# Second half's normalised tokens turned channel-major on VectorE and through DRAM, where TensorE turned them into PSUM

## The chip, the cores and the metric

The kernel runs on one core of one Trainium2 chip. The metric is device time in microseconds (us) of one execution, taken as the median of several runs; lower is better. In the profile the engines are called PE (TensorE, matrix products; PEld is its weight loading), DVE (VectorE), ACT (ScalarE), POOL (GpSimd) and SP (the sync engine, which here issues all DMAs, in program order). Every engine executes its own instructions strictly in the order in which the program issued them.

## The reference: what is computed

Input: x with 2048 tokens of 576 channels, all in float32. With `xn = layernorm(x)`, the result is

```python
out = x + A(xn, wqkv, wo) + B(xn, w1, b1, w2)
# A: qkv = xn @ wqkv, 32 heads of 18 channels; token s attends to tokens s, s-2, ..., s-14;
#    softmax over these 8 logits; the result @ wo
# B: mish(xn @ w1 + b1) @ w2, hidden width 4608
```

Both branches read the same normalised tokens `xn`. Every product with `xn` as an operand on TensorE needs it channel-major: 128 channels on the partitions, tokens along the free dimension. The input lies in DRAM token-major.

## The kernel before, in words

**Precision.** TensorE multiplies a reduced float format (fp32r in the profile). Each float32 operand is split into a high part (a cast by ACT) and a low part (the operand minus its high part, by DVE or POOL), and products are made as high·high + high·low + low·high. So for `xn` there are two channel-major copies, high and low, in one tile `XTs[hf, b]`.

**Tiling.** The tokens are taken in two halves (`hf` 0 and 1) of 1024; a half has two blocks (`b` 0 and 1) of 512 tokens, a block has four tiles (`jj`) of 128 tokens. Tile n = 4b + jj. The 576 channels are four groups of 128 (`KT` = 4) and a rest of 64. The rest is put twice into a 128-row group, so that its high part and its low part can share one operand; block 1 also needs the difference `rem` between the rests of block 0 and block 1, since some of the products are made by a seven-product scheme that works on sums and differences of blocks (`s_step`, `s_high` and `s_low` make these sums, tiles `S0` to `S2`; the sums run on POOL).

**The order of work.** TensorE's work is written out by hand as a list of slots, `plan`. A slot is one item for TensorE:

- `m`: a part of the up-projection of one pair of hidden groups q (0 to 17);
- `p`: a chunk of the down-projection, 24 products (L767), whose four results DVE adds to an accumulator (L771);
- `q`: 14 products that give one token tile's q, k and v for a group of heads (L348);
- `z`: the same for two groups of heads at once, by the seven-product scheme (L446);
- `t`: the turn of one tile of the second half (`ln_transpose(1, b, jj)`);
- `o`: the output projection.

Everything else is hung in front of a slot with `before(slot, function)`. In a slot the hung functions are issued first, in the order in which the program registered them, then mish of the part before, then TensorE's item. So a slot fixes the place of an instruction in its engine's queue, not its time. Attention runs on POOL (products L533 and L571) and DVE (sums L538 and L577), in steps hung in front of slots too.

**The turn of the second half, before.** Its tiles are loaded (`x_load`, L105) while the first half's last up-projection groups run, normalised by ACT in place (`norm1`, L139), and the rest of 64 channels is doubled by POOL (L140). In slot `t` TensorE transposes the tile against an identity, four groups of 128 channels into one PSUM bank (L75), the rest into another (L76) and, for block 1, `rem` too (L78). ACT casts from PSUM to the high part (L81, L86), DVE subtracts from PSUM to the low part (L82, L87). Two banks are taken for it: of tag "out" for the first three tiles of block 0 (`pair`), else of tag "h".

**The slots around the change.** E is the slot `t` of tile 3. The first column is the slot, the second TensorE's item, the third when that item began in the profile of before.

| slot | item | us |
|---|---|---|
| E-25 | chunk of q 14 | 471.78 |
| E-23 | first part of q 16 | 476.81 |
| E-21, E-19, E-17, E-15 | chunks of q 15 | 481.34, 485.89, 490.89, 495.89 |
| E-13 | first part of q 17, the last reader of the first half's block 0 | 500.89 |
| E-11, E-9, E-6, E-3 | chunks of q 16 | 505.42, 509.97, 515.54, 521.11 |
| E-8, E-5, E-2, E | `t` of tiles 0 to 3 | 513.15, 518.72, 524.29, 526.69 |
| E+1, E+2 | chunks of q 17 | from 527.15, without a gap |
| E+3, E+5, E+8, E+10 | second half's q items, block 0 | 533.61, 539.55, 546.07, 549.49 |
| E+4, E+6 | chunks of q 17; each chunk of q 17 is followed by two stores of finished accumulators (`y_store`, L1041) | 536.36, 542.31 |
| E+7, E+9, E+11, E+13 | `t` of tiles 4 to 7 | 545.50, 548.92, 552.34, 555.77 |
| E+12, E+14 to E+16 | q items, block 1, tiles 4 to 7 | 552.92, then from 556.35 without a gap |
| E+17 to E+24 | q items of the second group of heads | up to 586.73 |
| E+25 to E+28 | first four z items | 586.73, 589.49, 591.85, 595.29 |

The weights of the z items come by `z_fetch`, hung in front of E+14 to E+25, into buffers that other tiles have left: T2 into the four "raw" buffers, R3 into "r3", B11 and B21 into "acc". The sums `s_step(1, c, k)` are hung in front of E+14 to E+26.

**The way through DRAM that was there.** Attention's output is token-major too and is turned without TensorE: `o_turn` transposes every 32x32 block of a 128x576 tile on DVE (L593), `o_send` stores it by four DMAs in rows of 32 floats, 128 bytes, so that the blocks land in channel-major places (L602), and `o_load` reads it back in rows of 512 bytes (L892).

Of the kernel before, what the change touches and what calls it, by code (L numbers as in the profile page):

```python
# [21 lines left out]
TB = SH // NB  # L22
TJ = SH // P
JB = TJ // NB
KT = D // P
NF = F // P
NP = NF // 2
# [12 lines left out]
def block_kernel(ctx: ExitStack, tc: tile.TileContext, x, wq, wo, w1, b1, w2, mask, out):  # L40
    nc = tc.nc
    tpn = iter(range(1000))

    const = ctx.enter_context(tc.tile_pool(name="const", bufs=1))
    sb = ctx.enter_context(tc.tile_pool(name="sb", bufs=2))
    ps = ctx.enter_context(tc.tile_pool(name="ps", bufs=4, space=bass.MemoryType.PSUM))
    dram = ctx.enter_context(tc.tile_pool(name="dram", bufs=1, space=bass.MemoryType.DRAM))
# [16 lines left out]
    for k in range(30):  # L64
        nc.tensor.transpose(warm[:, (k % 4) * P:(k % 4 + 1) * P], ident, ident)

    def transpose_split(src, dst, col, extra=None, pair=False):
        n = next(tpn)
        if pair:
            ta, tb = (ps.tile([P, 512], F32, tag="out", bufs=4, name=f"tt{k}_{n}") for k in range(2))  # L70
        else:
            ta = ps.tile([P, 512], F32, tag="h", bufs=4, name=f"ta_{n}")
            tb = ps.tile([P, 512], F32, tag="h", bufs=4, name=f"tb_{n}")
        for k in range(KT):
            nc.tensor.transpose(ta[:, k * P:(k + 1) * P], src[:, k * P:(k + 1) * P], ident)  # L75
        nc.tensor.transpose(tb[:, 0:P], src[:, KT * P:(KT + 1) * P], ident)  # L76
        if extra is not None:
            nc.tensor.transpose(tb[:, P:2 * P], extra, ident)  # L78
        tav = ta.rearrange("p (k t) -> p k t", k=KT)
        hi = dst[:, 0:KT, col:col + P]  # L80
        nc.scalar.copy(hi, tav)  # L81
        nc.vector.tensor_sub(dst[:, 5:5 + KT, col:col + P], tav, hi.bitcast(F32))  # L82
        e = 1 if extra is None else 2
        hr = dst[:, KT:KT + 5 * e - 4:5, col:col + P]
        tbv = tb.rearrange("p (k t) -> p k t", k=KT)[:, 0:e]
        nc.scalar.copy(hr, tbv)  # L86
        nc.vector.tensor_sub(hr[64:P], tbv[64:P], hr[64:P].bitcast(F32))  # L87

    XTs = {}
    rems = {}  # L90
    xns = {}
    XNB = 5
# [7 lines left out]
    def x_tile(hf, n):  # L100
        return x[hf * SH:(hf + 1) * SH, :].rearrange("(p j) d -> p j d", j=TJ)[:, n, :]

    def x_load(n):
        xn = sb.tile([P, 5 * P], F32, tag="xn", bufs=XNB, name=f"xn_1_{n}_{next(tpn)}")
        nc.sync.dma_start(xn[:, 0:D], x_tile(1, n))  # L105
        xns[1, n] = xn

# [29 lines left out]
    def norm1(n):  # L137
        xn = xns[1, n]
        nc.scalar.activation(xn[:, 0:D], xn[:, 0:D], AF.Identity, bias=nm1[:, n, :], scale=rs1[:, n, :])  # L139
        nc.gpsimd.tensor_copy(xn[:, D:D + 64], xn[:, KT * P:D])  # L140

    group = {}

    def ln_group(ns):
# [39 lines left out]
    def ln_transpose(hf, b, jj):  # L184
        if jj == 0:
            XTs[hf, b] = sb.tile([P, 9 + b, TB], F32R, tag=f"xt{b}", bufs=1, name=f"xt_{hf}_{b}")
        xn = xns[hf, b * JB + jj]
        if (b, jj) == (0, 0):
            rems[hf] = sb.tile([P, JB, P], F32, tag="tt", bufs=2, name=f"rem_{hf}")
        rem = rems[hf][:, jj, :]  # L190
        if b == 0:
            nc.gpsimd.tensor_copy(rem, xn[:, KT * P:])
        else:
            nc.gpsimd.tensor_tensor(out=rem, in0=rem, in1=xn[:, KT * P:], op=ALU.subtract)
        transpose_split(xn, XTs[hf, b], jj * P, rem if b else None, (hf, b) == (1, 0) and jj < 3)

    def raw_load(src, width, name):
        raw = sb.tile([P, 5 * P], F32, tag="raw", bufs=4, name=f"r{name}")
# [176 lines left out]
    BUFS = {"wb": 3, "wc": 2, "wa0": 1, "a0": 3, "a1": 2, "acc": 9, "raw": 4, "tt": 2, "r3": 1, "mn": 5, "xn": XNB}  # L375
# [767 lines left out]
    at = {}  # L1143
# [3 lines left out]
    def add(tag, *fns, alias=None):  # L1147
        at[tag] = at[alias] = len(plan)
        plan.append((list(fns), [], PART[tag[3]] if tag[0] == "m" else US[tag[0]]))

    def before(i, fn):
        plan[max(i, 0)][1].append(fn)
# [70 lines left out]
            qkv_item(0, 0, 0, n)  # L1223

    def tr(b, jj):
        add(("t", 1, b, jj), lambda: ln_transpose(1, b, jj))

    CHUNKS = ((1, 0), (1, 1), (0, 0), (0, 1))

# [136 lines left out]
    for q in range(1, 2 * OC + 1):  # L1366
        i = spot(0, q, (3,2)[q > 1])
# [5 lines left out]
    i = spot(0, NP - 1, 0)  # L1373
# [5 lines left out]
    i = at["q", 1, 0, 1, 1]  # L1379
# [4 lines left out]
    i = spot(0, 9, 4)  # L1384
    for k in range(2):
        for n, steps in enumerate((
# [42 lines left out]
    i = at["q", 0, 1, 1, 0]  # L1429
# [3 lines left out]
    i = at["q", 0, 3, 1, 0]  # L1433
# [23 lines left out]
        before(i, lambda n=n: x_load(n))  # L1457
        before(i + 5, lambda n=n: stats1(n))
    before(i + 6, var1)
    i = spot(0, NP - 2, 0)  # L1460
    for jj in range(JB):
        before(i + 2 * jj, lambda jj=jj: x_load(jj))
        before(i + 2 * jj + 6, lambda jj=jj: norm1(jj))
        before(at["t", 1, 0, jj] + 2, lambda jj=jj: x_load(JB + jj))
    for jj in range(JB):
        before(at["p", 0, NP - 1, 1, 1] + jj, lambda jj=jj: norm1(JB + jj))

    for n, (name, pr) in enumerate((name, pr) for name in ("P4", "P5", "P2", "P3") for pr in range(2)):
        i = items[dict(P4=0, P5=2, P3=2, P2=3)[name]][2] + pr
# [125 lines left out]
```

## Time and profile before

| | before |
|---|---|
| runs | 1113.94, 1114.05, 1114.44 us, median 1114.05 |
| the profiled execution, whole | 1114.25 us |
| its span, first to last instruction | 1112.5 us |
| granted TensorE clock | 1.0 of full speed |
| share of the span busy: PE, PEld, DVE, ACT, POOL | 99%, 91%, 76%, 45%, 71% |
| DMA: mean rate, share of 16 engines' span | 244 GB/s, 71.6% |

How to read the views that follow: a group of instructions is given as line, engine, operation, output<-input, shape and count, then busy time and mean nanoseconds of one, then idle time of its engine in front of it and who ended it. A timeline row is start, duration, engine, line and a merged run of equal instructions ("x24"), with the wait in front of the run in brackets. TensorE's products are pipelined: the duration of a row reaches past the start of the next one, so what a row costs TensorE is the distance to the next start. Rows of SPq are DMAs being issued. A row of a window lists the length of the stretch, the busy time of each engine in it, the granted clock, the busy share of the DMA engines and what they moved.

### The profile page before, as it was taken

What the parts mean: (1) busy time and instruction counts of PE and PEld (TensorE: products, weight loads), DVE (VectorE), ACT (ScalarE), POOL (GpSimd) and SP (SyncE); (2) the same over time, 40 slices, a digit from 0 to 9 for tenths busy, and PEclk for the clock granted to TensorE, in tenths of its full rate; (3) what the DMA queues carried; (4) which work ended last, traced back from release to release, by engine and by line L of the source; (5) the groups of instructions that cost most, each with busy time, mean ns of one, the idle gap of its engine ahead of it and who ended that gap; (6) DMA issues with size and microseconds to landing.
All of it is one profiled execution on the core that took longest, in us unless ns stands there. A gap on an engine that the chain in (4) does not pass through costs nothing.

```text
span 1112.5 us, 18203 instructions
## 1 busy us (share of the span) xinstructions
PE 1101.6 (99%) x6550; PEld 1015.2 (91%) x6550; DVE 849.5 (76%) x1367; ACT 499.5 (45%) x917; POOL 790.8 (71%) x639
## 2 busy tenths in 40 slices
PE   9999999999999999999999999999999999999998
PEld 8999899999999999999999889989989999999998
DVE  6369788888889888897656577786776677777786
ACT  5544655544454544555333354433433344343353
POOL 2479777766679688785788676666688976867532
PEclk9999999999999999999999999999999999999999
DMA  6899696868777758675597898565664657776574
GB/s 202 283 312 316 225 356 214 285 233 276 258 242 264 268 208 301 249 249 204 190 323 241 245 375 307 211 196 196 220 222 170 209 195 223 244 288 219 171 232 142
DMA packets 178270, 271.60 MB, mean 244 GB/s; under 512 B 53218, under 2 KB 120068, under 8 KB 178180
## 3 DMA queue, kind: packets, MB, share of 16 engines
q1 hardware_dynamic: 178180, 270.44, 71.6%
q8 instruction: 52, 0.85, 0.3%
q14 instruction: 38, 0.31, 0.1%
HBM read 160.39 MB, written 110.00 MB: 243 GB/s over the span
## 4 chain that ended last, share of the span: by engine, by line
PE 87%; POOL 6%; DVE 3%; issue 2%; ACT 1%; DMA 0%; SPq 0%; POOLq 0%; DVEq 0%; ACTq 0%
PE h L669 28%; PE po L767 21%; PE pq L348 9%; PE po L880 9%; PE po L859 6%; PE h L675 5%; PE o L1063 5%; PE z L446 3%; POOL pv L571 2%; POOL accP L868 1%; POOL pr L533 1%; POOL act L721 1%; POOL s L620 1%; DMA acc<-in_x 0%; PE ta L75 0%
## 5 line engine op out<-in xcount | busy, mean ns | idle before, releaser
L767 PEld LDWEIGHTS po<-w,act 128*128 128x128 f32 x1728 | 236.4, 188 | 6.0 <-POOL act L721 0.4
L767 PE MATMUL po<-w,act 128*128 128x288 f32 x1728 | 240.7, 295 | 0.1
L533 POOL TENSOR_TENSOR pr<-q,kv 128x576 f32<-128x576 f32 x128 | 196.9, 1563 | 8.5 <-DMA q<-q_d 5.0
L721 POOL TENSOR_TENSOR act<-c,act 128x512 fp32r<-128x512 f32 x81 | 107.3, 1325 | 128.6 <-ACT act L720 128.6
L571 POOL TENSOR_TENSOR pv<-L,kv 128x576 f32<-128x576 f32 x128 | 177.9, 1484 | 26.1 <-DVE L L564 21.2
L771 DVE TENSOR_TENSOR acc<-po,acc 128x288 f32<-128x288 f32 x288 | 119.4, 448 | 29.9 <-PE po L767 29.0
L348 PE MATMUL pq<-wq,xt 128*128 128x432 f32 x672 | 136.5, 361 | 1.0 <-ACT xt L81 1.0
L880 PEld LDWEIGHTS po<-w,act 128*128 128x128 f32 x960 | 130.9, 188 | 4.6 <-DVE accP L883 1.8
L880 PE MATMUL po<-w,act 128*128 128x288 f32 x960 | 133.5, 295 | 1.0 <-DVE accP L883 1.0
L348 PEld LDWEIGHTS pq<-wq,xt 128*128 128x128 f32 x672 | 125.0, 188 | 8.0 <-ACT xt L81 1.8
L715 ACT ACTIVATE c<-c,b1c 128x512 f32<-128x512 f32 x81 | 58.7, 725 | 140.7 <-DVE c L714 140.4
L669 PE MATMUL h<-xt,t 128*128 128x512 f32 x432 | 110.6, 391 | 0.5 <-DVE rt L714 0.3
L669 PE MATMUL h<-S,t 128*128 128x512 f32 x432 | 110.5, 391 | 0.0
L577 DVE TENSOR_REDUCE og<-pv 128x144 f32<-128x1152 f32 x64 | 86.0, 1345 | 25.7 <-POOL pv L571 25.6
L669 PE MATMUL h<-xt,wa 128*128 128x512 f32 x432 | 104.1, 390 | 0.0
L538 DVE TENSOR_REDUCE L<-pr 128x64 f32<-128x1152 f32 x64 | 85.8, 1341 | 23.8 <-POOL pr L533 23.7
L703 ACT COPY c<-h 128x512 f32<-128x512 f32 x81 | 47.4, 586 | 124.1 <-PE h L675 73.0
L859 PEld LDWEIGHTS po<-pw,u 128*128 128x128 f32 x672 | 92.2, 188 | 5.4 <-DVE u L813 2.1
L859 PE MATMUL po<-pw,u 128*128 128x288 f32 x672 | 94.3, 295 | 2.5 <-DVE u L813 1.6
L669 PEld LDWEIGHTS h<-xt,wa 128*128 128x128 f32 x432 | 80.9, 188 | 17.0
L669 PEld LDWEIGHTS h<-xt,t 128*128 128x128 f32 x432 | 79.0, 188 | 15.7 <-DVE rt L714 0.7
L883 DVE TENSOR_TENSOR accP<-po,accP 128x288 f32<-128x288 f32 x160 | 68.9, 452 | 29.8 <-PE po L880 28.2
(228 smaller groups left out, 1853.8 us busy)
## 6 DMA issues: line engine op xcount, KB each, us to landing
kv<-kv_d SPq DMA_DIRECT2D x64, 396.0 KB, 5.1
kept_t<-t SPq DMA_DIRECT2D x36, 512.0 KB, 4.8
t<-kept_t SPq DMA_DIRECT2D x36, 512.0 KB, 6.7
rw<-in_w SPq DMA_DIRECT2D x36, 320.0 KB, 4.4
kept_wa<-wa SPq DMA_DIRECT2D x18, 640.0 KB, 4.7
kept_w<-w SPq DMA_DIRECT2D x20, 576.0 KB, 4.1
wa<-kept_wa SPq DMA_DIRECT2D x18, 640.0 KB, 5.2
w<-kept_w SPq DMA_DIRECT2D x20, 576.0 KB, 4.1
```

The lines of the kernel that those rows point to most:

```text
L348: nc.tensor.matmul(pq[:, 0:432], XT[:, xi, tok], wt[wi][:, hl, 0:432], start=i == 0, stop=i == len(seq) - 1)
L533: nc.gpsimd.tensor_tensor(out=pr[:, x:x + hh], in0=q[:, j0 + x:j0 + x + hh, None, :].to_broadcast([P, hh, W, CU]), in1=win(kt, 0, CU, j0 + ...
L538: nc.vector.tensor_reduce(L[:, k, j0:j0 + hj].rearrange("p j w h -> p (j w h)"), pr.rearrange("p j w (h d) -> p (j w h) d", h=2), axis=AX, ...
L571: nc.gpsimd.tensor_tensor(out=pr[:, x:x + hj].rearrange("p j d w -> p j w d"), in0=L[:, k, x:x + hj, :, h:h + 1].to_broadcast([P, hj, W, DH]),
L577: nc.vector.tensor_reduce(og[:, c0:c0 + DH, :].rearrange("p d j -> p j d"), pr, axis=AX, op=ALU.add)
L669: nc.tensor.matmul(ph, wt[:, wl, wk * P:(wk + 1) * P], X[:, xs, :], start=first and i == 0, stop=last and i == len(seq) - 1, skip_group_ch ...
L721: nc.gpsimd.tensor_tensor(out=a[:, 1, :], in0=t, in1=a[:, 0, :].bitcast(F32), op=ALU.subtract)
L767: nc.tensor.matmul(po, acts[hf, q, b, j][:, al, tok], done["w2", hf, 2 * q + j][:, wl, c * HC:(c + 1) * HC], start=i == 0, stop=i == 5)
L771: nc.vector.tensor_tensor(out=t, in0=po, in1=t, op=ALU.add)
L859: nc.tensor.matmul(po, units[e, k, qq][:, al, tok], w[:, qq, wl, :], start=i == 0, stop=i == 5)
L880: nc.tensor.matmul(po, acts[hf, q, b, j][:, al, tok], done["w2", hf, 2 * q + j][:, wl, c * HC:(c + 1) * HC], start=i == 0, stop=i == 5)
L883: nc.vector.tensor_tensor(out=t, in0=po, in1=t, op=ALU.add)
```

## The change

The eight `t` slots stay in the list but are empty. A second-half tile n now goes through six steps, each hung in front of a slot of its own:

1. `x_load`: as before, but tiles 4 to 7 go into "raw" buffers.
2. `norm1`: as before, without POOL's copy of the rest.
3. `x_turn`: DVE transposes the 32x32 blocks of the tile (128x576) into one of two buffers, by turns (one in the ninth "acc" buffer, one in "r3").
4. `x_put`: four DMAs store it in rows of 128 bytes in a DRAM tile [576 channels, 128 tokens].
5. `x_back`: one DMA reads the four groups of 128 channels, in rows of 512 bytes, and two more read the rest into both halves of a fifth group; the target is an "xn" buffer.
6. `x_high` and, a slot later, `x_low`: POOL copies the rest (block 0) or subtracts it (block 1) into `rem`; ACT casts from SBUF to the high part; DVE subtracts from SBUF to the low part. For block 1 the group of the rest and `rem` are cast and subtracted one by one.

The slots, relative to E:

| tile | load | norm | turn | put | back | high | low |
|---|---|---|---|---|---|---|---|
| 0 | -25 | -23 | -22 | -20 | -17 | -11 | -10 |
| 1 | -22 | -20 | -19 | -17 | -14 | -9 | -8 |
| 2 | -19 | -17 | -16 | -14 | -11 | -6 | -5 |
| 3 | -16 | -14 | -13 | -11 | -8 | -4 | -3 |
| 4 | -13 | -8 | -7 | -5 | 0 | +4 | +5 |
| 5 | -12 | -5 | -4 | -2 | +2 | +7 | +8 |
| 6 | -10 | -2 | -1 | +1 | +4 | +10 | +11 |
| 7 | -6 | +1 | +2 | +4 | +6 | +12 | +13 |

Before, the loads stood in front of E-23, -21, -19, -17, -6, -3, 0 and +2 and the normalisations in front of E-17, -15, -13, -11 and E+2 to +5. The first half's turns stay on TensorE.

```diff
-    def transpose_split(src, dst, col, extra=None, pair=False):
+    def transpose_split(src, dst, col, extra=None):
...
-        nc.gpsimd.tensor_copy(xn[:, D:D + 64], xn[:, KT * P:D])
+    def x_turn(n):
...
+        t = xTs["ab"[n % 2]]
+        nc.vector.transpose(t, xns[1, n][:, 0:D])
+    def x_put(n):
+        t = xTs[n]
+        d = xT_d[n] = dram.tile([D, P], F32, name=f"xT_d{n}")
+        rows = d.rearrange("(n i) p -> i n p", i=32)
+        for g in range(4):
+            part = slice(g * 32, (g + 1) * 32)
+            nc.sync.dma_start(rows[:, :, part], t[part].rearrange("i (n k) -> i n k", k=32))
+    def x_back(n):
+        xn = xns[1, n] = sb.tile([P, 5 * P], F32, tag="xn", bufs=XNB, name=f"xn_t_{n}")
+        nc.sync.dma_start(xn[:, 0:KT * P].rearrange("p (k t) -> p k t", k=KT),
+                          xT_d[n][0:KT * P].rearrange("(k p) t -> p k t", p=P))
+        for r_ in range(2):
+            nc.sync.dma_start(xn[r_ * 64:(r_ + 1) * 64, KT * P:], xT_d[n][KT * P:D])
+    def x_high(n):
...
+        if b == 0:
+            nc.gpsimd.tensor_copy(rem, xr)
+        else:
+            nc.gpsimd.tensor_tensor(out=rem, in0=rem, in1=xr, op=ALU.subtract)
+        for s_, hi, lo in x_parts(n):
+            nc.scalar.copy(hi, s_)
+    def x_low(n):
+        for k, (s_, hi, lo) in enumerate(x_parts(n)):
+            r_ = slice(64 if k else 0, P)
+            nc.vector.tensor_tensor(out=lo[r_], in0=s_[r_], in1=hi[r_].bitcast(F32), op=ALU.subtract)
...
     def tr(b, jj):
-        add(("t", 1, b, jj), lambda: ln_transpose(1, b, jj))
+        add(("t", 1, b, jj))
...
-    i = spot(0, NP - 2, 0)
-    for jj in range(JB):
-        before(i + 2 * jj, lambda jj=jj: x_load(jj))
-        before(i + 2 * jj + 6, lambda jj=jj: norm1(jj))
-        before(at["t", 1, 0, jj] + 2, lambda jj=jj: x_load(JB + jj))
-    for jj in range(JB):
-        before(at["p", 0, NP - 1, 1, 1] + jj, lambda jj=jj: norm1(JB + jj))
+    i, e = spot(0, NP - 3, 8), at["t", 1, 0, JB - 1]
+    for n in range(TJ):
+        b_, jj = divmod(n, JB)
+        turn = (e - 7, e - 4, e - 1, e + 2)[jj] if b_ else i + 3 * jj + 3
+        load_at = (e - 13, e - 12, e - 10, e - 6)[jj] if b_ else i + 3 * jj
+        split = e + (4, 7, 10, 12)[jj] if b_ else e + (-11, -9, -6, -4)[jj]
+        before(load_at, lambda n=n: x_load(n, "raw" if n >= JB else "xn"))
+        before(turn - 1, lambda n=n: norm1(n))
+        before(turn, lambda n=n: x_turn(n))
+        before(turn + 2, lambda n=n: x_put(n))
+        before(e + (0, 2, 4, 6)[jj] if b_ else turn + 5, lambda n=n: x_back(n))
+        before(split, lambda n=n: x_high(n))
+        before(split + 1, lambda n=n: x_low(n))
```

More of the change, by code (lines that the diff above doesn't have):

```diff
@@ L65, in block_kernel @@
         nc.tensor.transpose(warm[:, (k % 4) * P:(k % 4 + 1) * P], ident, ident)
-    def transpose_split(src, dst, col, extra=None, pair=False):
+    def transpose_split(src, dst, col, extra=None):
         n = next(tpn)
[L69 to L73, printed above, removed]
+        ta = ps.tile([P, 512], F32, tag="h", bufs=4, name=f"ta_{n}")
+        tb = ps.tile([P, 512], F32, tag="h", bufs=4, name=f"tb_{n}")
         for k in range(KT):
@@ L101, in x_tile, with x_load @@
         return x[hf * SH:(hf + 1) * SH, :].rearrange("(p j) d -> p j d", j=TJ)[:, n, :]
-    def x_load(n):
-        xn = sb.tile([P, 5 * P], F32, tag="xn", bufs=XNB, name=f"xn_1_{n}_{next(tpn)}")
+    def x_load(n, tag="xn"):
+        xn = sb.tile([P, 5 * P], F32, tag=tag, bufs=BUFS[tag], name=f"xn_1_{n}_{next(tpn)}")
         nc.sync.dma_start(xn[:, 0:D], x_tile(1, n))
@@ L194, in ln_transpose @@
             nc.gpsimd.tensor_tensor(out=rem, in0=rem, in1=xn[:, KT * P:], op=ALU.subtract)
-        transpose_split(xn, XTs[hf, b], jj * P, rem if b else None, (hf, b) == (1, 0) and jj < 3)
+        transpose_split(xn, XTs[hf, b], jj * P, rem if b else None)
     def raw_load(src, width, name):
```

17 lines of the change are left out of this document (added).

## The prediction

> **What bounds the kernel now.** First the page: the busy shares and the chain of waits.
>
> ```profile
> span 1112.5 us, 18203 instructions
> PE 1101.6 (99%) x6550; PEld 1015.2 (91%) x6550; DVE 849.5 (76%) x1367; ACT 499.5 (45%) x917; POOL 790.8 (71%) x639
> PE 87%; POOL 6%; DVE 3%; issue 2%; ACT 1%; DMA 0%; SPq 0%; POOLq 0%; DVEq 0%; ACTq 0%
> PE po L859 <- DVE u L813: 1.6, 1, 1.6
> ...
> PE h L669 <- DVE c L714: 0.2, 1, 0.2
> ```
>
> TensorE is busy for 99% of the span and is 87% of the chain. The last two lines are the first and the last of the nine rows that list all that TensorE waited for; the longest wait is 1.6 us, none lies at a turn of the second half. So work taken from TensorE shortens the kernel one for one, as long as nothing else comes late.
>
> **What the change removes.** The timeline of TensorE around a turn of block 0 and two of block 1:
>
> ```profile
> 508.60 1.53 PE L669 MATMUL h<-S,t 128*128 128x512 f32 x6
> 509.97 3.34 PE L767 MATMUL po<-w,act 128*128 128x288 f32 x24
> 513.15 0.60 PE L75 MATMUL tt<-ident,xn 128*128 128x128 f32 x4
> 513.58 0.27 PE L76 MATMUL tt<-ident,xn 128*128 128x128 f32 x1
> 513.61 1.63 PE L669 MATMUL h<-S,t 128*128 128x512 f32 x6
> 515.08 0.62 PE L675 MATMUL h<-xt,wc 128*128 128x512 f32 x2
> ...
> 533.61 2.92 PE L348 MATMUL pq<-wq,xt 128*128 128x432 f32 x14
> 536.36 3.35 PE L767 MATMUL po<-w,act 128*128 128x288 f32 x24
> ...
> 539.55 2.92 PE L348 MATMUL pq<-wq,xt 128*128 128x432 f32 x14
> ...
> 546.07 3.01 PE L348 MATMUL pq<-wq,xt 128*128 128x432 f32 x14
> 548.92 0.60 PE L75 MATMUL ta<-ident,xn 128*128 128x128 f32 x4
> ...
> 549.49 3.01 PE L348 MATMUL pq<-wq,xt 128*128 128x432 f32 x14
> ```
>
> Starts are what counts. The five transposes of block 0 hold TensorE from 513.15 to 513.61: 0.46 us. The six products behind them take 515.08 - 513.61 = 1.47, where the same six behind other products took 509.97 - 508.60 = 1.37: 0.10 more. Together 0.56 a tile. In block 1 it is 549.49 - 548.92 = 0.57, and the fourteen products behind a turn take 548.92 - 546.07 = 2.85 against 536.36 - 533.61 = 2.75: 0.67 a tile. Four of each: 4 x 0.56 + 4 x 0.67 = **4.92 us less on TensorE**, 2.24 of them before E+1, 2.68 from E+7 to E+14. No wait of TensorE hangs on them, so nothing further is won.
>
> **What it adds on VectorE.** The groups of the nearest instructions and the busy times by stage:
>
> ```profile
> L255 DVE TENSOR_TENSOR t<-tt,t 128x512 fp32r<-128x512 f32 x36 | 45.1, 1254 | 4.3 <-ACT t L254 4.2
> L593 DVE STREAM_TRANSPOSE oT<-og 128x576 f32<-128x576 f32 x16 | 12.4, 773 | 0.3
> L82 DVE TENSOR_TENSOR xt<-ta,xt 128x512 fp32r<-128x512 f32 x13 | 9.0, 690 | 11.6 <-ACT xt L81 11.5
> L87 DVE TENSOR_TENSOR xt<-tb,xt 64x256 fp32r<-64x256 f32 x8 | 3.4, 428 | 0.2
> L87 DVE TENSOR_TENSOR xt<-tb,xt 64x128 fp32r<-64x128 f32 x5 | 1.5, 294 | 0.2
> ```
> ```profile
> 480.00:500.00 20.00, 20.00 (x130) 18.71 (x129) 19.19 (x29) 8.89 (x15) 17.03 (x15) 1.00 0.82 289
> 500.00:513.00 13.00, 13.00 (x78) 11.82 (x77) 10.67 (x15) 7.88 (x12) 7.64 (x8) 1.00 0.49 182
> 513.00:533.00 20.00, 20.00 (x139) 18.92 (x138) 15.38 (x31) 10.40 (x19) 12.20 (x14) 1.00 0.62 211
> 533.00:556.00 23.00, 23.00 (x145) 22.20 (x144) 13.91 (x22) 6.27 (x17) 16.17 (x17) 1.00 0.60 187
> 556.00:580.00 24.00, 24.00 (x126) 22.95 (x125) 13.29 (x15) 9.68 (x26) 21.11 (x17) 1.00 0.99 328
> 580.00:600.00 20.00, 19.86 (x102) 18.66 (x101) 12.28 (x14) 6.30 (x19) 18.07 (x14) 1.00 1.00 316
> ```
>
> A turn is the same instruction and shape as attention's L593: 0.773 us. The subtraction of four groups moves from PSUM (L82, 0.690) to SBUF. The nearest row from SBUF is L255, 1.254: 0.564 more; the other end is no more at all. The rest costs 2 x 0.294 in block 1 against 0.428.
>
> From 480 to 533, DVE idles 0.81 + 2.33 + 4.62 = 7.76 us; TensorE's 2.24 less shorten that to 5.52. Into it go the turns of tiles 0 to 6, 7 x 0.773 = 5.41, and four subtractions, 0 to 2.26: 5.41 to 7.67 in a room of 5.52. Between -0.1 and 2.15 us do not fit. What is late then is L771, the addition that frees the banks of a down-projection chunk, and TensorE waits for a free bank; the chunks at E+1 and E+2 follow each other without a gap, so it shows there. I take the middle, **+1.0 us**. From 533 on DVE idles 9.09 us, 6.41 after the shortening, and is given 0.77 + 4 x (0.564 + 0.16) = 3.7: nothing. ACT casts what it cast before. A normalisation of block 0 now stands two slots behind its load, where it stood six; a late load stops ACT and the copies behind it that empty the up-projection's banks. ACT idles for 11.1 of the 20 us from 480, which hides that: nothing, and without that cover as much as the load is late.
>
> **What it adds on the DMA queue.** The nearest transfers, attention's store and load of the same shape, a window that held little but one such store, one that held large transfers, and the z stage's last weights:
>
> ```profile
> 482.00:484.75 2.75, 2.75 (x22) 2.71 (x21) 2.75 (x4) 1.54 (x3) 2.75 (x2) 1.00 0.84 117
> 486.00:490.00 4.00, 4.00 (x30) 3.83 (x29) 4.00 (x6) 1.00 (x2) 4.00 (x3) 1.00 1.03 408
> ```
> ```profile
> 481.36 1.98 SPq L602 DMA_DIRECT2D o_d<-oT  x4
> ...
> 584.77 0.90 SPq L421 DMA_DIRECT2D z_T<-kept_T  x2
> ```
> ```profile
> zraw_T<-kept_T SPq DMA_DIRECT2D x4, 216.0 KB, 6.4
> o<-o_d SPq DMA_DIRECT2D x16, 320.0 KB, 5.7
> o_d<-oT SPq DMA_DIRECT2D x64, 72.0 KB, 2.6
> ```
> ```profile
> 593.42 1.34 PE L446 MATMUL z<-z_T,xt 128*128 128x432 f32 x6
> ```
>
> A store of a tile takes SP 1.98 us to issue, lands 2.6 us behind the last issue, and holds the DMA engines for 0.84 x 2.75 = 2.31 us. Reading back moves 320 KB in rows of 512 bytes: 0.8 us at the 408 GB/s of the second window, 2.8 at the 117 of the first. I take 1.0, near the fast end, since these rows are four times as long. Eight tiles: 8 x 3.3 = 26.5 us of DMA time. From 480 to 556 the engines were busy for 16.4 + 6.4 + 12.4 + 13.8 = 49.0 us; with the new work 75.4, in 76 - 4.9 = 71.1 us. Up to 4.3 us spill past E+14, into a stage at a share of 0.99 and 1.00. There the weights T4 are issued at 584.77, land by the 6.4 of their nearest row at 591.2, and TensorE needs them at 593.42: 2.2 us to spare. So TensorE waits there for 0 to 2.1 us.
>
> The same lateness meets a second path: in the chain of waits from 565 to 595 stand POOL's sums L620 for the same z items, which need the tiles of block 1.
>
> ```profile
> 537.97 0.24 POOL L140 COPY xn<-xn 128x64 f32<-128x64 f32 x1 [5.32 <-ACT xn L139]
> ...
> 552.57 1.30 POOL L620 TENSOR_TENSOR s<-xt 128x512 f32<-128x512 f32 x1
> ```
> ```profile
> 569.91 1.36 POOL s L620
> ...
> 595.29 24.82 PE z L446 x125
> ```
>
> POOL loses L140 and its wait of 5.32, so it can be early; but its `rem` of tile 7 now waits for `x_back`. That is issued behind the stores of chunk E+4, which ends at 539.55 - 2.24 = 537.3; an addition later and 2 us of SP make it 540, and 5.7 to land 545.7, with the spill up to 550. The sums began at 552.57 and have to begin 4.9 earlier, at 547.7: 0 to 2.3 us late. Both paths end in the same z items, so they are one term: 0 to 2.3, and I take **+0.6**, since the spill counts every transfer as if none could wait for a gap.
>
> **The sum.** -4.92 + 1.0 + 0.6 = -3.3 us. The profiled execution took 1114.25 us, 0.2 above the median of 1114.05; against the median the forecast is 1110.7. By the lower bounds of both terms 1109.1, by the upper ones 1113.6. About 0.2% (2.2 us) is what this measurement can tell from no change.
>
> [...] TensorE makes a 128x128 block here in about 0.11 us (513.15 to 513.58 for four), DVE only blocks of 32x32 and then a store. [...]
>
> **The rivals.**
>
> *All of the room is found* (chance 0.12): DVE's queue takes the turns in its idle time and the spill finds gaps. For it: from E-13 to E-11 no chunk stands, so lateness there costs nothing. Time: 1109.1.
>
> *Both engines are full* (0.15): subtractions cost 1.254 throughout, as POOL is busy, and the whole spill reaches z. For it: DVE's 19.19 of 20 us at 480. Against: 9 us of its idle time behind 533. Time: 1113.6, within 0.2% of before.
>
> *The round trip holds up SP, slower* (0.22): `x_back` waits in SP's queue until the store in front of it has landed, and everything behind it, y stores, attention's loads and the weights of the q items, waits too. A trip held up by the one before adds 1.98 + 2.6 + about 1.5 = 6.1 us. If that happens once in block 1 on top of the full spill, tile 7 lands at 545.7 + 4.3 + 6.1 = 556.1, 8.4 behind the 547.7 at which POOL's sums must begin, and TensorE waits as long in z: -4.9 + 1.0 + 8.4 = +4.5, 1118.5. It becomes slower than before when tile 7 lands after 552.6. Against: two to five slots lie between each store and its read, so SP seldom meets a store that is still on its way.
>
> *The store breaks into elements* (0.01): one packet of the store takes 2.31 x 16 / 2304 = 16 ns of one DMA engine; at 4 bytes instead of 128 a tile has 32 times as many, 74 us, and the kernel would take over 1600 us. Against: L602 has the same form and its packets are 128 bytes long.
>
> **How the numbers follow.** The forecast keeps 0.50, 1109.1 to 1113.6 with most of it under 1111.8. Faster by over 0.2%: 0.50 + 0.12 = 0.62. Within: 0.15. Slower: 0.22 + 0.01 = 0.23. The range leaves out the upper half of the slow case and the tip of the fast one: 1109.0 to 1117.0.
>
> **What would show it.** Right: no L75 after 500 us; z beginning 3 to 5 us earlier than 586.73; eight DVE transposes at 0.77 us more; waits of L767 at E+1 and E+2 for L771 of about a microsecond; SBUF subtractions between 0.69 and 1.25. Wrong: waits of L348 for the subtraction or the cast, of L446 for POOL, DVE or a DMA above 2.3 us, or a z stage that begins no earlier.

## The result, and the profile after

| | before | after |
|---|---|---|
| median (runs) | 1114.44 us (7: 1113.94 to 1114.96) | 1117.86 us (7: 1116.44 to 1118.22) |
| profiled execution, its span | 1114.25, 1112.5 | 1118.04, 1116.2 |
| TensorE's start into z, and out of it | 586.73, 624.88 | 589.34, 628.24 |

The changed kernel is slower: ratio 1.0029, 95% interval 1.0019 to 1.0039. The forecast was 1110.7 and its range ended at 1117.0. "Out of z" is the start of the first up-projection row behind the z items; it serves below as a cleaner measure than the time, since the stretch behind it holds one more wait, around 820, that varies from run to run; each value is from one profiled execution.

The page of after, and what TensorE waited for between 465 and 640 (total, times, longest). One row is left out, 0.7 us for L749; before has it too, for L703, and nothing else:

```profile
PE 1099.9 (99%) x6506; PEld 1011.8 (91%) x6506; DVE 858.5 (77%) x1379; ACT 499.7 (45%) x921; POOL 790.8 (71%) x631
...
PE po L813 <- DVE acc L817: 2.9, 1, 2.9
PE z L492 <- DVE zqs L505: 0.9, 1, 0.9
PE pq L394 <- DMA wq<-kept_wq: 0.9, 3, 0.4
PE po L813 <- POOL act L767: 0.8, 1, 0.8
```

TensorE's share is still 99%, but 3.8 us of standstill now lie at one place that had none. The timeline of TensorE in before, the last part of the up-projection and the first row behind z:

```profile
526.23 0.62 PE L675 MATMUL h<-xt,wc 128*128 128x512 f32 x2
624.88 2.93 PE L669 MATMUL h<-xt,wa 128*128 128x512 f32 x12
```

And in after, from the last part of the up-projection to the first q item, and at z:

```profile
524.26 0.62 PE L721 MATMUL h<-xt,wc 128*128 128x512 f32 x2
527.83 0.53 PE L813 MATMUL po<-w,act 128*128 128x288 f32 x2 [2.95 <-DVE acc L817]
529.18 7.90 PE L813 MATMUL po<-w,act 128*128 128x288 f32 x46 [0.82 <-POOL act L767]
536.92 3.10 PE L394 MATMUL pq<-wq,xt 128*128 128x432 f32 x14
...
589.34 2.51 PE L492 MATMUL z<-zacc_B,xt 128*128 128x432 f32 x12
598.66 1.43 PE L492 MATMUL z<-z_B,S 128*128 128x432 f32 x6 [0.91 <-DVE zqs L505]
628.24 2.93 PE L715 MATMUL h<-xt,wa 128*128 128x512 f32 x12
```

Before, 7.38 us lay between the last part (526.23) and the first q item (533.61); now 12.66 (524.26 to 536.92). 3.77 of it are the two waits in brackets. A further 1.6 are in the row of 46 products: it took 7.74 us to the next start, where 46 of 48 products take 6.46 x 46/48 = 6.2. The windows show why; the column behind the five engines is the granted clock, 0.88, 0.50 and 0.76:

```profile
528.00:530.00 2.00, 1.18 (x6) 0.94 (x7) 1.77 (x2) 1.97 (x4) 2.00 (x2) 0.88 0.82 246
530.00:532.00 2.00, 2.00 (x10) 2.00 (x10) 0.75 (x2) 0.54 (x1) 2.00 (x3) 0.50 1.06 220
532.00:534.00 2.00, 2.00 (x14) 2.00 (x14) 0.69 (x3) 0.00 (x0) 2.00 (x3) 0.76 0.97 295
```

The whole difference, from starts of TensorE in both timelines: -1.97 us at the last part, +5.28 from there to the first q item, -0.70 over the q items (where the turns of block 1 had stood with 2.68, so some 2.0 were lost again, 0.9 of it in waits for `wq`), +0.75 in z, +0.34 behind it. Together +3.70, as the spans say (1116.2 - 1112.5). So the saving of the turns is there, and more than it is given back at three places.

VectorE, by stage, in the windows whose rows the prediction shows for before:

```profile
533.00:556.00 23.00, 23.00 (x143) 22.17 (x142) 18.23 (x28) 5.77 (x20) 15.01 (x14) 1.00 0.93 261
556.00:580.00 24.00, 23.11 (x115) 20.91 (x114) 19.12 (x18) 8.11 (x23) 21.96 (x17) 1.00 1.06 344
```

From 533 to 556 it was busy for 13.91 us and is now for 18.23, from 556 to 580 for 13.29 and now 19.12. That is 10.1 us more, where the prediction had put 3.7. The subtractions of block 1 make 8.0 of it (12.5 us for its four tiles against 4.5) and a turn 0.8; the rest is other work that came later than before and so fell into these windows. In the timeline of VectorE of before:

```profile
526.12 0.68 DVE L82 TENSOR_TENSOR xt<-tt,xt 128x512 fp32r<-128x512 f32 x1
557.08 0.69 DVE L82 TENSOR_TENSOR xt<-ta,xt 128x512 fp32r<-128x512 f32 x1 [0.90 <-ACT xt L81]
557.80 0.43 DVE L87 TENSOR_TENSOR xt<-tb,xt 64x256 fp32r<-64x256 f32 x1
```

The same in after:

```profile
514.66 1.00 DVE L185 TENSOR_TENSOR xt<-xn_t,xt 128x512 fp32r<-128x512 f32 x2
518.44 2.13 DVE L185 TENSOR_TENSOR xt<-xn_t,xt 128x512 fp32r<-128x512 f32 x2
553.08 3.31 DVE L185 TENSOR_TENSOR xt<-xn_t,xt 128x512 fp32r<-128x512 f32 x2 [0.28 <-ACT xt L180]
556.32 1.38 DVE L185 TENSOR_TENSOR xt<-rem,xt 64x128 fp32r<-64x128 f32 x1
```

Before, the 128x512 subtraction took 0.68 or 0.69 us wherever it stood. Now it and the small one behind it (one row of two, 1.00 at 514.66) take 2.13 at 518.44, and tile 6 takes 3.31 + 1.38, where a tile of block 1 took 0.69 + 0.43. GpSimd's timeline beside the last ones, of before:

```profile
556.44 2.82 POOL L533 TENSOR_TENSOR pr<-q,kv 128x576 f32<-128x576 f32 x2
```

And of after, with the first of its sums for z:

```profile
552.97 3.28 POOL L579 TENSOR_TENSOR pr<-q,kv 128x576 f32<-128x576 f32 x2
556.21 1.34 POOL L666 TENSOR_TENSOR s<-xt 128x512 f32<-128x512 f32 x1
```

GpSimd worked beside the subtraction at 557.08 of before too, and it did not grow. That subtraction read one operand from PSUM; the new ones read both from SBUF. The third thing that is late is a tile; ScalarE's timeline of after, the cast of tile 3:

```profile
523.98 0.82 ACT L180 CAST xt<-xn_t 128x512 fp32r<-128x512 f32 x2 [4.16 <-DMA xn_t<-xT_d]
```

ScalarE and all that is queued on it stood for 4.16 us until the tile had come back from DRAM.

### The profile page after: what moved, and what is told of

Same layout as the page of the kernel before. It is cut to its first block, busy times and chain, and to the rows that moved or that the text cites. A ratio compares the mean times of both kernels' runs of the same rounds, so it can differ in the third digit from the quotient of the medians.

```text
span 1116.2 us, 18218 instructions
## 1 busy us (share of the span) xinstructions
PE 1099.9 (99%) x6506; PEld 1011.8 (91%) x6506; DVE 858.5 (77%) x1379; ACT 499.7 (45%) x921; POOL 790.8 (71%) x631
## 4 chain that ended last, share of the span: by engine, by line
PE 83%; POOL 6%; DVE 6%; issue 3%; ACT 2%; DMA 1%; SPq 0%; DVEq 0%; POOLq 0%; ACTq 0%
PE h L715 27%; PE po L813 20%; PE po L926 9%; PE pq L394 8%; PE po L905 6%; PE h L721 5%; PE o L1109 4%; PE z L492 3%; POOL pv L617 2%; POOL accP L914 1%; DVE xt L185 1%; POOL pr L579 1%; POOL act L767 1%; POOL s L666 1%; DVE L L584 1%
## 5 line engine op out<-in xcount | busy, mean ns | idle before, releaser
L617 POOL TENSOR_TENSOR pv<-L,kv 128x576 f32<-128x576 f32 x128 | 178.1, 1486 | 27.4 <-DVE L L610 22.8
L817 DVE TENSOR_TENSOR acc<-po,acc 128x288 f32<-128x288 f32 x288 | 118.9, 448 | 28.4 <-PE po L813 27.5
L584 DVE TENSOR_REDUCE L<-pr 128x64 f32<-128x1152 f32 x64 | 85.8, 1342 | 25.9 <-POOL pr L579 25.8
L749 ACT COPY c<-h 128x512 f32<-128x512 f32 x81 | 47.4, 585 | 120.2 <-PE h L721 71.2
```

Source lines behind the costliest of these rows:

```text
L584: nc.vector.tensor_reduce(L[:, k, j0:j0 + hj].rearrange("p j w h -> p (j w h)"), pr.rearrange("p j w (h d) -> p (j w h) d", h=2), axis=AX, ...
L617: nc.gpsimd.tensor_tensor(out=pr[:, x:x + hj].rearrange("p j d w -> p j w d"), in0=L[:, k, x:x + hj, :, h:h + 1].to_broadcast([P, hj, W, DH]),
L817: nc.vector.tensor_tensor(out=t, in0=po, in1=t, op=ALU.add)
```

## The experiments

All stand against runs of the kernel before on the same chip. "Out of z" is the offset of that start against 624.88 in the one profiled execution of each. A, B, C, Q, L, V, S and G are the theories of the expectations: A and L say that tiles come back late, B and V that VectorE is full, C and Q that SP's queue or the DMA engines are, S blames the subtraction from SBUF, G GpSimd's sums ahead of z.

| run | ratio, 95% interval | out of z |
|---|---|---|
| after | 1.0029 [1.0019, 1.0039] | +3.36 |
| e1 tile 3 split late | 1.0041 [1.0028, 1.0053] | +3.77 |
| e2 block 1 alone through DRAM | 1.0005 [0.9997, 1.0014] | -1.00 |
| e3 block 0 alone through DRAM | 1.0023 [1.0015, 1.0032] | +1.38 |
| e4 stores issued by ScalarE | 1.0099 [1.0086, 1.0112] | +9.77 |
| e5 trip not waited for | 1.0029 [1.0018, 1.0040] | +3.19 |
| e6 no stores and reads | 1.0019 [1.0010, 1.0029] | +2.23 |
| e7 no turns either | 1.0008 [0.9999, 1.0017] | +0.12 |
| e8 before, with 56 idle DMAs | 1.0000 [0.9991, 1.0010] | -0.42 |
| e9 no subtractions, whole trip | 1.0019 [1.0009, 1.0030] | +1.50 |
| e10 no subtractions, no trip | 0.9955 [0.9940, 0.9970] | -4.43 |
| e11 before, subtracting from SBUF | 1.0019 [1.0010, 1.0029] | +2.04 |
| e12 tiles 0, 1, 4, 5 through DRAM | 0.9991 [0.9981, 1.0001] | -1.53 |
| e13 no subtractions, trip not waited for | 1.0019 [1.0009, 1.0028] | +1.98 |
| e14 stores issued by GpSimd | 1.0586 [1.0570, 1.0601] | not compared |

**e1 to e4: where does it lie?** The first four asked for the place.

```diff
-        split = e + (4, 7, 10, 12)[jj] if b_ else e + (-11, -9, -6, -4)[jj]
+        split = e + (4, 7, 10, 12)[jj] if b_ else e + (-11, -9, -6, 3)[jj]      # e1
```

e2, and e3 with 1 in place of 0:

```diff
-        add(("t", 1, b, jj))
+        if b == 0:
+            add(("t", 1, b, jj), lambda: ln_transpose(1, b, jj))
+        else:
+            add(("t", 1, b, jj))
...
+        if b_ == 0:
+            continue
```

That block's loads and normalisations stand at their old slots; `rem` then takes a difference of a token-major and a channel-major rest, so it holds other values than the layer's. e4:

```diff
-            nc.sync.dma_start(rows[:, :, part], t[part].rearrange("i (n k) -> i n k", k=32))
+            nc.scalar.dma_start(rows[:, :, part], t[part].rearrange("i (n k) -> i n k", k=32))    # e4; e14 with nc.gpsimd
```

> The changed kernel with the split of tile 3 alone moved from E-4 and E-3 to E+3 and E+4 (it is first needed at E+10). Theory A, one late read: ACT reached the cast of tile 3 before its read had landed, waited 4.2 us, DVE behind it waited 2.1 us, so the additions of chunk E-3 and mish came late and TensorE stood still for 2.95 and 0.82 us and then ran at a lowered clock. Then this kernel is free of both waits, its clock is 1.00 in all stretches, and the 5.8 us lost between E and E+3 come back: about 1112. Rival B, DVE is full: the work on DVE is the same, so a wait of L817 of 2 us or more stays at E+1: 1116 to 1118. Rival C, SP and the DMA engines are full: the wait at E+1 goes, but TensorE arrives earlier at the fetches of the q weights and waits there for what it gained: about 1116.

> Block 0 turned on TensorE as before the change, block 1 through DRAM as after it. Theory A: nothing waits at E-4, TensorE saves the 2.68 us of block 1 and loses about 1.7 us to the late q weights and 0.8 to DVE in z as in the changed kernel: 1113.5 to 1114.5, granted clock 1.00. Rival B: DVE has 9 us of idle time where block 1 is turned, so all is kept: 1111.8. Rival C: SP has 14 us less to issue before E, so the weights are in time too: 1112.

> Block 0 through DRAM as after the change, block 1 turned on TensorE as before it. Theory A: the read of tile 3 is still late, though less since SP no longer issues the loads of tiles 4 to 6 and the store of tile 4 ahead of it: TensorE saves 2.24 us and loses 2 to 6: 1114 to 1118, with a wait of ACT for xn_t at E-4. Rival B: five of eight turns on DVE fall in the full stretch, a wait of L817 at E+1 of 1 to 3 us: 1113 to 1116, without a wait of ACT for xn_t. Rival C: 1112.2, since SP has room.

> The changed kernel with the four store DMAs of each tile issued by ACT's queue in place of SP's, all at the same slots. The DMA engines move the same, SP issues 32 fewer, ACT 32 more. If SP's issue time is what made the read of tile 3 late (theory A's first cause), the read lands 3 us or more earlier, the waits at E-4 and E+1 shrink to under 1 us and the q weights come in time: 1110 to 1113. If the DMA engines' own time made it late, it lands as late as before: 1116 to 1118. If ACT cannot take the issues (about 2 us a tile), takes and mish come late and TensorE waits in the up-projection between E-20 and E: over 1118.

e1 took the casts and the subtraction of tile 3 out of the way of E+1. The wait there fell from 2.95 to 0.50 us, and the time did not. The two rows that bear on it, of what TensorE waited for in e1 between 465 and 640 (beside them 1.7 us stand in z and 0.7 for L749):

```profile
PE pq L394 <- DMA wq<-kept_wq: 4.0, 3, 3.2
PE po L813 <- DVE acc L817: 0.5, 1, 0.5
```

The q item at E+3 came early, at 532.10, and stood 3.2 us for its weights. Theory A, by which the late tile was all, fell: under one wait lay another, the one that C had named. e2 and e3 say that both blocks lose, block 0 more: of 2.68 us that block 1 saves, 1.0 arrive behind z, and of block 0's 2.24 nothing does. e4 moved the stores to an engine whose own order they hold up: TensorE waited 5.7 us for VectorE's additions and 1.5 for ScalarE's copies. No wait for the weights is left in it, but with TensorE so late that says little on SP.

**e5 to e8: the trip taken apart.** In e5 to e7 the casts, the subtractions and `rem` read the resident 128x128 identity; then the DMAs go, then the turns.

```diff
-        return [(xn[:, 0:KT * P].rearrange("p (k t) -> p k t", k=KT), dst[:, 0:KT, cs], dst[:, 5:5 + KT, cs]),
+        return [(ident.unsqueeze(1).to_broadcast([P, KT, P]), dst[:, 0:KT, cs], dst[:, 5:5 + KT, cs]),   # e5, e6, e7
...
-        before(turn + 2, lambda n=n: x_put(n))                                     # e6, e7
-        before(e + (0, 2, 4, 6)[jj] if b_ else turn + 5, lambda n=n: x_back(n))    # e6, e7
-        before(turn, lambda n=n: x_turn(n))                                        # e7
```

e8 adds to the kernel before, at the slots of `x_put` and `x_back`:

```diff
+            nc.sync.dma_start(rows[:, 0:4, part], ident[part].rearrange("i (n k) -> i n k", k=32))    # four times
...
+            nc.sync.dma_start(idle_d[n][P * (r_ + 1):P * (r_ + 1) + 64], ident[0:64])                   # three times
```

> Every turn, store and read of the round trip is issued as in the changed kernel, but the casts, the subtractions and GpSimd's rest read the resident 128x128 identity in place of the tile that comes back, so nothing waits for a read. (What is split is the identity, so the output is not the layer's.) In the changed kernel SP's queue issued for 74.9 of the 80 us from 480 to 560, against 41.0 before. Theory Q, SP's queue is full, and so whatever it issues is late, the reads and the weights alike: the standstill at E+1 goes, but the weights of the q items at E+3 are still issued 7 to 12 us later than before, so TensorE waits for them there, about 3 us as with tile 3 split late; time 1113 to 1116. Theory L, only the waits for the reads cost: 1109.5 to 1111. Theory V, VectorE is full with turns and subtractions: waits for the additions of L817 remain, time as the changed kernel's 1117.9.

> As the run before, and the stores and the reads are left out too; the turns on VectorE stay. (The identity is split, so the output is not the layer's.) Q and L: all weights come in time, TensorE keeps its 4.92 us, 1109.3 to 1110.5. Theory G, GpSimd's sums and attention between 550 and 597 are a second bound that ends z no more than about 1 us earlier than before: TensorE reaches z 4 to 5 us earlier and waits there for 2 to 4 us, time 1111 to 1113. V: 1115 or more.

> As the run before, without the eight turns on VectorE (8 x 0.77 = 6.2 us of its time). (The identity is split, so the output is not the layer's.) V: at least 2 us faster than the run before. Q, L and G: within 0.7 us of it, since VectorE's room takes the turns.

> The kernel before with its transposes on TensorE, and at the slots of the round trip's stores and reads 7 small DMAs a tile from the identity to DRAM that nothing reads or waits for: 4 of 32x128 elements in rows of 128 bytes, 3 of 64x128; some 0.25 us of DMA time a tile, but 56 more issues on SP's queue. Q: some 28 us more of SP's issuing between 480 and 556, weights of the q items issued several us later, TensorE waits for a DMA before or in the q items: 1115.5 to 1118. L, V and G: SP's issuing alone costs nothing, 1114.0 to 1114.8.

No theory gave all four times. V's fit e5, e6 and e8, but by it e7 should be at least 2 us faster than e6; it was 1.1 faster by the medians (2.1 by "out of z"), and with no DMA and no turn left it was still no faster than before, though TensorE had 4.92 us less to do. L fell with e5 (the reads not waited for, the same time). The chain of waits of e7, from the q items to z (start, us, engine, tile, line; pieces under 0.1 us left out):

```profile
549.84 1.81 DVE xt L185
551.68 2.73 DVE xt L185 x2
554.43 1.35 DVE L L584
555.78 1.71 DVE xt L185
557.53 2.85 DVE xt L185 x2
...
571.33 2.96 POOL pv L617 x2
...
589.07 2.94 POOL pv L617 x2
...
594.12 0.65 DVE S L702
...
595.41 4.78 PE z L492 x23
```

It goes through the subtraction L185 of tiles 6 and 7 on VectorE, 3.3 and 3.2 us for what two undisturbed instructions do in 0.97, with 1.4 and 1.5 for the one on `rem`; behind them attention's L584, behind that GpSimd, and so z. Block 0's saving was gone at E+1, where TensorE waited 1.0 us for L817 and 0.8 for GpSimd: the first q item began at 533.84, against 533.61 before. Block 1's was gone in z: TensorE reached it at 584.35, 2.4 us earlier than before, and left it 0.12 later. What was left to blame was the subtraction itself (S).

e8 put the count of issues to the test, with few of the bytes: the single issues took SP 62.6 of the 80 us from 480 to 560 (30.8 before, 66.6 after; the 41.0 and 74.9 of e5's expectation add up timeline rows, which merge several issues with the pauses between them), and nothing was late. A queue that is busy with small DMAs is not what costs here (1.0000). By their shapes they move 160 KB a tile, where the trip moves 608; no run shows the 0.25 us of DMA time a tile that e8's expectation names.

**e9 to e12: the subtraction.**

```diff
-            nc.vector.tensor_tensor(out=lo[r_], in0=s_[r_], in1=hi[r_].bitcast(F32), op=ALU.subtract)
+            nc.scalar.copy(lo[r_], s_[r_])                                         # e9 on after, e10 on e7
```
```diff
-        nc.vector.tensor_sub(dst[:, 5:5 + KT, col:col + P], tav, hi.bitcast(F32))
+        nc.vector.tensor_sub(dst[:, 5:5 + KT, col:col + P], ident.unsqueeze(1).to_broadcast([P, KT, P]) if hf else tav, hi.bitcast(F32))   # e11 on before
```

e12 leaves the trip to the pairs of tiles (0, 4) and (1, 5) and gives the others back to TensorE, with their loads and normalisations at the old slots:

```diff
+        if jj in (0, 1):
+            add(("t", 1, b, jj))
+        else:
+            add(("t", 1, b, jj), lambda: ln_transpose(1, b, jj))
...
+        if jj not in (0, 1):
+            continue
```

> The changed kernel with the whole round trip, but L185's subtraction on VectorE is left out and ScalarE writes the same low parts by one more cast (the low part holds the value's high part again, so the output is not the layer's). Theory S, what costs is the subtraction with both operands in SBUF: it takes 0.97 to 1.0 us a tile where GpSimd rests, 1.9 to 2.4 from 518 to 528 and 4.6 to 4.7 from 550 to 560, where GpSimd works beside it; in the run without DMAs and turns it still held up L760 at E+1 and GpSimd's sums ahead of z. S: E+1's wait falls below 1.5 us and GpSimd's sums begin at least 2 us earlier than 556.2; with the late reads and weights still there, 1112 to 1115. Theory Q, a full queue of SP: 1116 to 1118 as before. Theory V, the turns: 1116 to 1118.

> The run without DMAs and turns (the identity is split), with the low parts written by ScalarE as in the run before. S: nothing is left but TensorE's 4.92 us and a lower bound from GpSimd's sums: 1109.5 to 1112. If the sums of GpSimd bind by themselves (theory G): 1113 to 1115, near the 1115.7 with the subtractions.

> The kernel before, with its transposes on TensorE and its casts from PSUM; only the subtractions of the second half's tiles take the identity in SBUF in place of the transposed tile in PSUM (so the output is not the layer's). No DMA, no turn, no slot is moved. S: the same 18 subtractions take 1.9 to 4.7 us a tile beside GpSimd instead of 0.97 to 1.12, z waits for VectorE or GpSimd, 1116 to 1119. Q, V and G: 1114.0 to 1114.8, since the operand's place is no load.

> Tiles 0, 1, 4 and 5 take the round trip at the changed kernel's slots, tiles 2, 3, 6 and 7 stay on TensorE as before; nothing is left out. In the run without DMAs the subtractions of 0, 1, 4 and 5 ran beside a resting GpSimd, in 0.97 to 1.0 us. TensorE has 2 x 0.56 + 2 x 0.67 = 2.46 us less. S: the saving stays, 1111.6 to 1112.8, faster than before. Q: half the issues, some waits for weights, 1112.5 to 1114. G: block 1's half is given back at z, 1113 to 1114.

e10 against e7 changes the subtraction alone: 0.9955 against 1.0008, and out of z 4.55 us earlier. All that TensorE waited for in e10 from 465 to 640:

```profile
PE h L715 <- ACT rt L749: 0.7, 1, 0.7
```

Its rows at E+1 and at z:

```profile
525.07 6.92 PE L813 MATMUL po<-w,act 128*128 128x288 f32 x48
582.33 2.52 PE L492 MATMUL z<-zacc_B,xt 128*128 128x432 f32 x12
```

E+1 now follows the last part without a gap, z begins 4.4 us earlier than before, and most of the 4.92 us that the prediction had taken from TensorE is there: 4.43 behind z, and 5.0 by the ratio (3.3 to 6.7 by its interval, of the 1115.72 that the kernel before took in this set). So the subtraction is what held e7 up, and G as a bound by itself falls: GpSimd's sums follow VectorE and begin at 549.18, against 552.92 in e7. But e10 takes all 17.7 us of subtractions from VectorE, and before has 8.4 there; it does not say that their place is at fault. e11 does: nothing but the operand's place is changed in the kernel before, the same sixteen instructions (its expectation says 18) take 17.8 us in place of 8.4, TensorE waits 1.0 us for L771 and 1.3 in z where it had waited for neither, and 2.04 us are lost. VectorE's timeline of e11, tile 7, with GpSimd at work:

```profile
557.98 1.77 DVE L82 TENSOR_TENSOR xt<-ident,xt 128x512 fp32r<-128x512 f32 x1
559.78 1.54 DVE L87 TENSOR_TENSOR xt<-ident,xt 64x256 fp32r<-64x256 f32 x1
```

1.77 and 1.54 us, where the rows of before, above, have 0.69 and 0.43 at 557.08 and 557.80. GpSimd's sum had begun at 557.90, 0.08 us ahead, and took 1.30, where the same sum took 1.28 in before (at 555.20). Which of the two grew went with their order. Tile 6 of e11, VectorE's row and GpSimd's beside it:

```profile
554.56 0.69 DVE L82 TENSOR_TENSOR xt<-ident,xt 128x512 fp32r<-128x512 f32 x1 [0.25 <-ACT xt L81]
554.60 1.80 POOL L620 TENSOR_TENSOR s<-xt 128x512 f32<-128x512 f32 x1
```

Here the subtraction began first and took its 0.69, and GpSimd's sum took 1.80, where the same sum took 1.30 in before (at 552.57).

e9 missed what S had expected: the whole trip without subtractions is no faster than 1.0019. So each of the two is enough by itself to lose the saving, the subtractions in e7 and the trip here. TensorE waited there 2.1 us at E+1, for ScalarE and GpSimd, and 3.4 for the weights of the q items. e12 was to keep half of the tiles clear of GpSimd's busy stretches, at 1111.6 to 1112.8 by S, and missed too. Its subtractions of tiles 0 and 1 took 1.00 us each, those of 4 and 5 still 3.3 and 2.4, and z gave 1.3 us back:

```profile
PE z L497 <- DVE zqs L510: 1.3, 1, 1.3
```

It is the fastest whole kernel here and is not told apart from before. Behind z it was 1.53 us ahead; its profiled execution then has the longer of the two waits at 820 (below), and five of its runs took 1113.1 to 1113.8 us, the other six 1115.4 to 1116.6.

**e13 and e14: what in the trip costs 6 us.** e13 is e5 with e9's line; e14 is e4's line with `nc.gpsimd`.

> The changed kernel with every turn, store and read issued, nothing waiting for a read (the identity is split) and the low parts written by ScalarE. It stands between e9 (the reads waited for, no subtraction: 1.0019 of before) and e10 (no trip, no subtraction: 0.9955). Theory L, e9's loss is in the tiles that come back late: 0.995 to 0.998, close to e10, 1109.5 to 1112. Theory Q, it is SP's queue and the weights behind it: 0.999 to 1.002, 1113.5 to 1116.5, with waits for wq of 3 us or more in the q items as in e9.

> The changed kernel with its 32 stores issued from GpSimd's queue instead of SP's; nothing else moves and nothing is left out. Theory Q: SP issues for some 20 us less between 480 and 560, and the weights of the q items at E+3 and behind 557 come in time, so TensorE waits for no wq; but GpSimd's own work is delayed by 32 issues of 0.5 to 0.6 us, which its sums ahead of z cannot take: 1115 to 1119. Theory S beside it: the subtractions stay slow, so it cannot come below 1115. Theory L alone: under 1114.

e13 waits for no tile and subtracts nothing, and is as slow as e9. What TensorE waited for ahead of z in e13, in `wq`:

```profile
PE pq L394 <- DMA wq<-kept_wq: 4.0, 1, 4.0
```

SP's rows for these weights in e13:

```profile
531.80 0.39 SPq L328 DMA_DIRECT2D wq<-kept_wq  x1
533.96 0.53 SPq L328 DMA_DIRECT2D wq<-kept_wq  x1
```

And in e10:

```profile
517.42 0.67 SPq L328 DMA_DIRECT2D wq<-kept_wq  x1
519.78 5.80 SPq L328 DMA_DIRECT2D wq<-kept_wq  x2
```

Of the five weights, e13 issues the last two at 531.80 and 533.96, e10 within 519.78 to 525.58, and TensorE stands in e13 for 4.02 us at E+3. e8 issued its last two at 523.16 and 526.47, though SP was as busy ahead of them: from 505 to 534 its single issues took 22.8 us in e8 (46 issues) and 22.9 in e13 (39). Together this points to the bytes that the DMAs move and not to their count; it does not show it, since e8 and e13 also differ in the turns and in the slots of the loads. Whether it is the DMA engines (busy share 0.90 to 0.99 in the changed kernel from 500 to 556, against 0.49 to 0.62 before) or the longer issues that come with them (a tile's store 2.2 to 3.7 us in e13, against 1.8 to 3.2 in e8) was not separated.

e14 missed by 60 us. A store on GpSimd's queue, in its own timeline:

```profile
488.35 0.88 POOL L152 DMA_DIRECT2D xT_d<-xT_a  x1
494.40 0.68 POOL L152 DMA_DIRECT2D xT_d<-xT_a  x1 [5.18 <-issue]
497.01 0.67 POOL L152 DMA_DIRECT2D xT_d<-xT_a  x1 [1.93 <-issue]
```

Some 0.7 us of issuing for each of four stores a tile, and 1.9 us or more in front of the second, third and fourth, 64.8 us of such pauses from 480 to 600, on an engine with 21 of 24 us busy ahead of z. So it could not show whether SP was relieved.

## Why the prediction was wrong, step by step

- *What is removed, 4.92 us.* Right in size: e10 has 4.43 of it behind z. That "work taken from TensorE shortens the kernel one for one, as long as nothing else comes late" held too; its condition failed.
- *The subtraction, +0.564 us a tile at most: this is the first of two steps that failed.* "The nearest row from SBUF is L255, 1.254" is a mean over 36 instructions, and it was taken as an upper end. The line's own instructions in the trace of before (minimum, median and maximum in ns) have:

```profile
L255 DVE TENSOR_TENSOR t<-tt,t x36: 682/1292/1781, 94.5 to 495.9; 128x512 fp32r<-128x512 f32 x36
```

  From 0.68 to 1.78: the upper end stood there, 1.1 us above the price from PSUM and not 0.564, and the smaller instructions of a tile stretch too. In the new kernel tile 6 takes 3.31 + 1.38 = 4.69 against 0.69 + 0.43 = 1.12. Block 0's four tiles took 5.0 us against 3.9, inside the 0 to 2.26; block 1's took 12.5 against 4.5, 2.0 more a tile where 0.564 + 0.16 was the most. e11 shows +2.04 us behind z from the operand's place alone; e10 against e7 shows 4.55 for the whole subtraction. Which of the two engines loses the time went with their order: in e7 the subtraction from 549.84, 0.16 us behind the start of two GpSimd products, took 1.81; in e11 the one from 554.56, 0.04 ahead of GpSimd's sum, took 0.69, and the sum was the one that grew, to 1.80. What holds the later one up was not shown. The forecast's own sum has no term for what GpSimd does beside the subtraction.
- *"From 533 on ... nothing."* Wrong for the same reason: 8.0 us more for the subtractions, not 4 x (0.564 + 0.16) = 2.9, and they stand ahead of L584 and GpSimd's sums, so idle time elsewhere does not hide them. The sums began at 556.21, where the prediction wanted 547.7 for the whole saving; e10, which kept 4.43 us, has them at 549.18.
- *The place of the lateness, E+1.* Right, but +1.0 was 3.77 of standstill, and behind it TensorE's clock fell to 0.50, 1.6 us that no term held. In e6, where no tile comes late, the wait for L817 is 2.20, the top of the 0 to 2.15; the 0.8 for GpSimd behind it and the clock were left out there too.
- *DMA: up to 4.3 us that spill into z.* The second step that failed, in its path. The time of the DMA engines was about right (75.4 us from 480 to 556; 0.92 of 76, some 70, were found), but the harm came at another place: TensorE never waited for T4, and it waited for the weights of the q items (0.9 us in after, 4.0 in e13 and in e1). By e9 and e13 the trip alone, with no subtraction, makes the kernel slower than before (1.0019). Everything that SP issues behind the stores should have been listed.
- *ScalarE, "nothing".* The late tile 3 did stop ScalarE for 4.16 us, but e5 removes that and gains nothing: VectorE was almost as late anyway (2.2 us of waits for L817 against 2.9).
- *The rivals.* "The round trip holds up SP", 1118.5, gave the time within 0.7 us, with a sum start 8.4 us late where 8.5 were found. That is luck, since its mechanism is not what the runs show: in after SP never waited more than 0.7 us for a store of the trip, and e7, without any trip, still has sums at 552.92. That the weights of the q items would be late it did say. "Both engines are full" had the mechanism, its subtractions at 1.254 throughout, and too small a price.

## What to carry to other kernels

Ask of every operand that moves from PSUM to SBUF what GpSimd does at that time: with GpSimd at work beside it, tile 7's 128x512 subtraction took 0.69 us from PSUM (before, 557.08) and 1.77 from SBUF (e11, 557.98); a group's mean hides it (L255, 1254 ns), its minimum and maximum show it (682 and 1781). Before calling room free, follow it to the end. Two delays that TensorE meets one behind the other can overlap: time lost at the first, E+1, was no longer lost at the second, the weights of the q items (2.95 and 0.9 us in after, 0.50 and 4.0 in e1). Out of z, against e10, the subtractions alone cost 4.6 us (e7), the trip with its turns 6.4 (e13), both 7.6 (e5) and not 11; so undoing one gains 1.2 or 3.1, and only the run that undoes both shows what each was worth. And moving work off an engine that is 99% busy was worth its time here only up to the next engine's slack (of 4.92 us, 4.43 were kept in e10, and after was 3.36 late): measure that slack at the stage, not over the span.

## What was not expected of the hardware

After a standstill of 2.95 us in after, and of 2.20 at the same place in e6, TensorE was granted 0.50 of its clock for 2 us and more (530 to 532 in both); after 2.13 us in e3 it kept 1.00 (524 to 538). Late in the span, a down-projection of e3 behind a wait of 2.4 us:

```profile
820.09 4.93 PE L910 MATMUL po<-pw,u 128*128 128x288 f32 x24 [2.40 <-ACT rm L766]
```

The same place in e9:

```profile
820.72 3.44 PE L905 MATMUL po<-pw,u 128*128 128x288 f32 x24 [2.41 <-ACT rm L761]
```

Two like rows of 24 products with the same wait in front, 4.93 and 3.44 us long; from 822 to 824 the granted clock was 0.50 in e3 and 1.00 in e9 (over the span 0.998 and 1.0). What decides it was not shown. The length of the standstill alone does not: the clock fell after 2.20 and 2.40 us and held after 2.13 and 2.41. The wait at 820 itself was 0.8 to 0.9 us in most of the profiled runs, before, after and e10 among them, and 2.4 in e1, e3, e9 and e12; why it has two lengths is not shown.
